# A linear-attention and gated-MLP kernel ordered anew, with one more step transposed by DMA

## The chip, the cores and the metric

The kernel runs on one core of one Trainium2 chip. A time is the device time of one execution in microseconds (us); the number that counts is the median of several runs. The core has the engines TensorE (PE, matmuls), VectorE (DVE), ScalarE (ACT), GpSimd (POOL) and SyncE (SP), which here issues nearly all DMAs. They work side by side, each through its own list of instructions in order, and wait for one another by semaphores.

## The reference

Two layers. The first is attention with a decaying state (4 batches, 8 heads, 768 positions, head size 64):

```python
for b in range(nb):                      # blocks of 64 positions
    intra = np.einsum('bhic,bhjc->bhij', qb, kb) * Dmask[None]
    intra = np.einsum('bhij,bhjd->bhid', intra, vb)
    inter = np.einsum('bhid,bhde->bhie', qb * lam_pow[None], kv_state)
    out[:, :, sl] = intra + inter
    kv_state = lam_block[None, :, None, None] * kv_state + np.einsum('bhsd,bhse->bhde', kb_dec, vb)
```

The second takes its output x (4 x 768 x 512) through a gated MLP that mixes positions:

```python
h = np.maximum(x @ w_in, 0.0)            # 512 -> 1024
u, v = (h[..., :d_ff // 2].copy(), h[..., d_ff // 2:].copy())
v_n = (v - mu) / np.sqrt(var + 1e-06)    # over the last axis
v_s = np.einsum('ts,bsd->btd', w_spatial, v_n) + b_spatial[None, :, None]
return ((u * v_s) @ w_out).astype(np.float32)
```

## The kernel before

The positions are cut into 12 steps of 256 (three to a batch; n = 0 to 11), each two chunks of 128. A step goes through these pieces; the name is the one in the table that orders them, the L number the line in the kernel before.

- Loads (LK, LQ, LV; L194): k, q and v of the step, 512 KB each, on SP's queue, into three buffers each in turn. Weights come in between (WH, WQ, WP) and are cast to bf16 (CW, CX, WC, WX).
- Scaling (KM, QM; L329): k and q times the decay, into kc and qc in bf16, on POOL or DVE. VC casts v (POOL or ACT).
- Transposing: kT and qT, two buffers each. Steps 0 to 5 do it on PE (TK, TQ; L364: eight 128x128 transposes for k and eight for q, halves of four where the piece has a half number 0 or 1, and an eviction EK or EQ). Steps 6 to 11 do it by a DMA on SP's queue (DK, L342; DQ, L346).
- Attention in 64x64 pieces of PE's array: scores (SC, L394, 16 matmuls a half), masked by DVE (MK, L399); state products (KP, L423) with the sums SX, SY, SA; outputs (AV, L457 with the state and qT, L466 with the masked scores). EX moves them to xT.
- First MLP products: PV (L491, four 512-wide matmuls a chunk) and PU (L542, eight 256-wide), evicted with the ReLU by EV and EU. BN, RA, RD, RB, VN normalise v.
- After three steps, a batch's second half: PW (L568, the spatial product, eight groups of six 384-wide matmuls, each started on a bank into which GP has put the bias), GM (DVE, the gate), PO (L579, six output tiles of four 512-wide matmuls; PH, L588, a half tile), EO and the store ST.
- FL (L307): products of a tile of ones whose results nobody reads.

What runs when is a hand-made table, ORDER, of tokens such as `SC.3.1.3.4.T`: the piece, its step and half, its PSUM banks (3 and 4) and the engine that does it (T for PE, D for DVE, A for ACT, P for POOL, S for SP). The program walks through the table once and issues each piece, so that the table gives every engine its list. Semaphore waits follow from the data. The tile `ps` is all eight PSUM banks; which bank a piece gets decides whose eviction it waits for.

Of the kernel before, what the change touches and what calls it, by code (L numbers as in the profile page):

```python
# [16 lines left out]
lam.A BR.A tab.0.A LK.0.S LQ.0.S LV.0.S LQ.1.S LK.1.S LK.2.S LV.1.S LQ.2.S WH.0.S WH.1.S posk.P idn.P msk.P one.D  # L17
row.D FL.1.256.4.1.T FL.1.512.1.1.T FL.1.256.0.1.T FL.1.256.3.1.T FL.1.256.3.1.T FL.1.512.3.1.T FL.1.512.6.1.T
LB.6.T FL.1.256.1.1.T FL.1.256.4.1.T FL.1.256.3.1.T BB.1.5.T BB.0.2.T LN.6.A LL.D mkc.D LX.A QM.0.0.P TQ.0.0.1.T
KM.0.0.D KM.0.1.D QM.0.1.P TK.0.0.0.T TK.0.1.4.T TQ.0.1.3.T EK.0.0.0.D QM.1.0.D QM.1.1.D BE.1.5.A BE.0.2.A  # L20
EQ.0.0.1.A EK.0.1.4.A VC.0.P SC.0.0.0.1.T EQ.0.1.3.A KP.0.6.T SC.0.1.4.5.T TQ.1.0.2.T TQ.1.1.3.T KM.1.1.P KM.1.0.P
MK.0.0.0.1.D KM.2.1.P KM.2.0.P VD.1.1.P TK.1.1.0.T EQ.1.0.2.A SX.0.A EK.1.1.0.A VD.1.0.A MK.0.1.4.5.D EQ.1.1.3.D
FL.1.256.2.1.T TK.1.0.1.T SC.1.1.2.3.T eps.D SY.0.6.D EK.1.0.1.D MK.1.1.2.3.D QM.2.1.P CW.0.P CW.1.P AV.0.0.6.1.T
SC.1.0.4.5.T TK.2.1.0.T TK.2.0.2.T FN.0.6.1.A SA.0.1.D AV.0.1.6.1.T KP.1.3.T EK.2.0.2.A EX.0.0.6.A MK.1.0.4.5.D
AV.1.0.2.6.T QM.2.0.D TQ.2.1.5.T TQ.2.0.4.T FN.1.2.6.A EX.0.1.1.A SA.1.0.D EK.2.1.0.D AV.1.1.2.6.T EQ.2.0.4.A
EQ.2.1.5.D SY.1.3.D CW.2.D CW.3.D EX.1.1.6.A EX.1.0.2.A SC.2.1.0.1.T SC.2.0.4.5.T PV.0.0.3.T PV.0.1.6.T PV.1.0.2.T
EV.0.0.3.A EV.0.1.6.A LV.2.S MK.2.0.4.5.D MK.2.1.0.1.D SA.1.1.D WH.3.S LK.3.S WH.2.S LQ.3.S PV.1.1.5.T VC.2.P
KP.2.6.T AV.2.0.3.6.T CX.1.D PU.1.1.4.T GP.0.0.0.0.A tab.1.A FN.2.3.6.A EV.1.0.2.A SA.2.0.D AV.2.1.3.6.T PU.0.1.1.T
EX.2.0.3.A EX.2.1.6.A KM.3.1.P KM.3.0.P BN.0.1.D BN.0.0.D EV.1.1.5.D BN.1.1.D RA.0.A GP.0.3.0.2.D BN.1.0.D
EU.1.1.4.A PV.2.0.3.T EU.0.1.1.A EV.2.0.3.A PV.2.1.6.T EV.2.1.6.A WQ.1.S WQ.0.S RD.0.D BN.2.0.D RA.1.A RD.1.D  # L30
BN.2.1.D WC.0.D WQ.2.S WC.2.D CX.0.P QM.3.1.P QM.3.0.P TK.3.2.4.T PU.0.0.3.T EK.3.2.4.A EU.0.0.3.A PU.1.0.5.T
TQ.3.2.1.T PU.2.1.6.T WC.1.P RA.2.A RB.0.D RD.2.D LQ.4.S WQ.4.S WQ.5.S WQ.3.S LV.3.S LK.4.S EQ.3.2.1.A EU.2.1.6.A
WT.1.0.4.T WT.0.0.3.T WT.2.0.1.T PU.2.0.6.T EW.0.0.3.A VN.0.0.D VN.1.1.D VN.2.0.D EW.1.0.4.D VN.1.0.D VN.0.1.D
VN.2.1.D EW.2.0.1.A EU.2.0.6.A GP.0.2.0.6.A EU.1.0.5.A WC.4.A SC.3.1.3.4.T PW.0.0.0.0.T PW.0.3.0.2.T PW.0.2.0.6.T
MK.3.1.3.4.D WC.5.D GN.2.1.P GP.0.1.1.5.D GM.0.0.0.0.D QM.4.0.P WC.3.P GM.0.2.0.6.D GM.0.3.0.2.D WT.0.1.4.T
WT.2.1.0.T WT.1.1.1.T EW.2.1.0.D EW.1.1.1.D GP.0.1.0.3.A EW.0.1.4.A GP.0.0.1.6.A QM.4.1.P KM.4.0.P KM.4.1.P WP.S
WX.0.P PW.0.1.0.3.T LV.4.S VC.4.P VC.3.A GM.0.1.0.3.D GP.0.2.1.2.A PW.0.0.1.6.T SC.3.0.0.1.T KP.3.4.T TQ.4.2.3.T
PW.0.2.1.2.T GM.0.0.1.6.D EQ.4.2.3.A WX.1.A GP.0.3.1.6.D SY.3.4.D MK.3.0.0.1.D PW.0.3.1.6.T PW.0.1.1.5.T TK.4.2.0.T
PO.0.2.3.T EO.0.2.3.A SA.3.1.D SX.3.D GM.0.2.1.2.D GM.0.3.1.6.D GM.0.1.1.5.D EK.4.2.0.D LQ.5.S QM.5.1.D QM.5.0.P
LK.5.S KM.5.0.P KM.5.1.P PO.0.0.1.T AV.3.0.2.3.T EO.0.0.1.A LV.5.S KP.4.6.T SC.4.1.4.5.T FN.3.2.3.D AV.3.1.2.3.T  # L40
SY.4.6.D SC.4.0.0.1.T PO.0.3.6.T EX.3.1.3.A TQ.5.2.3.T MK.4.1.4.5.D EQ.5.2.3.A EX.3.0.2.D PV.3.1.4.T TK.5.2.5.T
VC.5.P LK.7.S LV.6.S LK.6.S EO.0.3.6.D MK.4.0.0.1.D SA.4.0.D SA.4.1.D EK.5.2.5.A PV.3.0.2.T AV.4.0.6.3.T EV.3.1.4.A
EV.3.0.2.A FN.4.6.3.D SC.5.0.0.1.T KP.5.6.T AV.4.1.6.3.T SC.5.1.4.5.T PU.3.0.2.T EX.4.0.6.A EX.4.1.3.A PV.4.0.6.T
BN.3.1.D MK.5.0.0.1.D MK.5.1.4.5.D SA.5.0.D BN.3.0.D KM.6.0.P KM.6.1.P LQ.7.S KM.7.0.P QM.7.0.P PV.4.1.0.T
PU.4.0.1.T AV.5.0.3.4.T FN.5.3.4.D EU.3.0.2.A VC.6.A EV.4.1.0.A EV.4.0.6.A KP.6.5.T AV.5.1.3.4.T RA.3.A RD.3.D
# [596 lines left out]
```

## Time and profile before

| | before |
|---|---|
| runs | 142.14, 140.97, 142.09 us; median 142.09 |
| span of the profiled execution | 140.7 us |
| PE busy | 133.6 us (95%), 1977 matmuls |
| DVE busy | 114.0 us (81%) |
| ACT, POOL busy | 77.2 us (55%), 60.6 us (43%) |
| mean granted PE clock | 0.988 |
| moved by DMA | 34.12 MB, mean 242 GB/s |

The time of the profiled execution itself isn't listed beside its span. The span runs from its first to its last instruction; the runs were between 0.3 and 1.4 us longer. Busy shares are means over stages with different limits: in the first 17 us the loads are what everything waits for, later PE has hardly a gap.

### The profile page before, as it was taken

What the parts mean: (1) busy time and instruction counts of PE and PEld (TensorE: products, weight loads), DVE (VectorE), ACT (ScalarE), POOL (GpSimd) and SP (SyncE); (2) the same over time, 40 slices, a digit from 0 to 9 for tenths busy, and PEclk for the clock granted to TensorE, in tenths of its full rate; (3) what the DMA queues carried; (4) which work ended last, traced back from release to release, by engine and by line L of the source; (5) the groups of instructions that cost most, each with busy time, mean ns of one, the idle gap of its engine ahead of it and who ended that gap; (6) DMA issues with size and microseconds to landing.
All of it is one profiled execution on the core that took longest, in us unless ns stands there. A gap on an engine that the chain in (4) does not pass through costs nothing.

```text
span 140.7 us, 4687 instructions
## 1 busy us (share of the span) xinstructions
PE 133.6 (95%) x1977; PEld 85.6 (61%) x1977; DVE 114.0 (81%) x234; ACT 77.2 (55%) x149; POOL 60.6 (43%) x70
## 2 busy tenths in 40 slices
PE   5998879999999999999999999999999999999990
PEld 2575664778676657657666465686565666756630
DVE  1549959999989798689888978999799599985470
ACT  3264555799875369758712068684313558781111
POOL 5178664940998169900861139915802000000000
PEclk9999968999999999999999999999999999999999
DMA  3999999999999999996903799999936550025285
GB/s 84 347 347 347 386 362 363 396 373 340 368 339 317 294 271 346 236 227 202 333 26 78 166 344 372 355 229 258 158 75 57 196 203 0 5 78 220 94 303 201
DMA packets 56729, 34.12 MB, mean 242 GB/s; under 512 B 13827, under 2 KB 51971, under 8 KB 56708
## 3 DMA queue, kind: packets, MB, share of 16 engines
q1 hardware_dynamic: 56560, 33.69, 82.7%
q8 instruction: 15, 0.25, 0.7%
q10 hardware_dynamic: 148, 0.13, 0.3%
q14 instruction: 6, 0.05, 0.1%
HBM read 24.38 MB, written 6.29 MB: 218 GB/s over the span
## 4 chain that ended last, share of the span: by engine, by line
PE 84%; SPq 6%; DMA 5%; POOL 1%; issue 0%; ACT 0%; POOLq 0%
PE ps L568 22%; PE ps L491 15%; PE ps L542 15%; PE ps L579 14%; SPq L194 6%; DMA q_in<-in_q_dram 5%; PE ps L394 4%; PE ps L466 4%; PE ps L364 3%; PE ps L457 3%; PE ps L423 2%; PE ps L554 1%; POOL qc L329 1%; PE ps L588 1%; ACT o_sb L179 0%
## 5 line engine op out<-in xcount | busy, mean ns | idle before, releaser
L568 PE MATMUL ps<-wt_sb,vn 128*128 128x384 bf16 x192 | 32.9, 326 | 0.0
L399 DVE TENSOR_TENSOR a_sb<-ps,m 128x1024 bf16<-128x1024 f32 x24 | 28.5, 1215 | 2.7 <-PE ps L394 1.7
L329 POOL TENSOR_TENSOR kc<-k_in,lv 128x512 bf16<-128x512 f32 x22 | 22.9, 1063 | 14.6 <-PE ps L423 5.2
L568 PEld LDWEIGHTS <-vn 128*128 128x128 bf16 x192 | 18.4, 98 | 12.0
L329 POOL TENSOR_TENSOR qc<-q_in,lqn 128x512 bf16<-128x512 f32 x20 | 21.5, 1094 | 4.7 <-DMA q_in<-in_q_dram 4.6
L542 PE MATMUL ps<-xT,win_sb 128*128 128x256 bf16 x192 | 23.5, 273 | 0.0
L491 PE MATMUL ps<-win_sb,xT 128*128 128x512 bf16 x96 | 23.4, 384 | 0.0
L579 PE MATMUL ps<-wout_sb,gT 128*128 128x512 bf16 x92 | 21.7, 379 | 0.0
L542 PEld LDWEIGHTS <-win_sb 128*128 128x128 bf16 x192 | 18.2, 98 | 4.0 <-DVE xT L181 0.2
L574 DVE TENSOR_TENSOR gT<-ps,uT 128x384 bf16<-128x384 f32 x32 | 16.6, 551 | 3.8 <-PE ps L568 3.7
L179 ACT ACTIVATE o_sb<-ps 128x512 f32<-128x512 f32 (+1 forms) x14 | 7.6, 565 | 16.6 <-PE ps L579 10.1
L506 DVE BATCH_NORM_STATS2 st<-vh 128x6 f32<-128x512 bf16 x24 | 16.3, 680 | 0.1
L183 POOL CAST vb<-v_in 128x1024 bf16<-128x1024 f32 (+1 forms) x10 | 9.9, 995 | 13.6 <-PE ps L466 7.8
L179 ACT ACTIVATE ps<-bsp 128x384 f32<-128x384 f32 x23 | 10.9, 487 | 7.7 <-DVE gT L574 5.1
L491 PEld LDWEIGHTS <-xT 128*128 128x128 bf16 x96 | 9.0, 99 | 9.7 <-ACT xT L179 1.0
L496 ACT ACTIVATE vh<-ps 128x512 bf16<-128x512 f32 x19 | 11.1, 595 | 6.3 <-PE ps L491 5.9
L579 PEld LDWEIGHTS <-gT 128*128 128x128 bf16 x92 | 8.6, 98 | 9.2
L179 ACT ACTIVATE xT<-ps 128x512 bf16<-128x512 f32 x20 | 11.1, 593 | 5.0 <-PE ps L466 4.2
L181 DVE COPY o_sb<-ps 128x512 f32<-128x512 f32 x11 | 7.6, 688 | 4.1 <-PE ps L579 3.6
L496 ACT ACTIVATE uT<-ps 128x512 bf16<-128x512 f32 x17 | 9.8, 590 | 1.2 <-PE ps L542 1.1
L394 PE MATMUL ps<-qT,kT 64*64 64x128 bf16 x384 | 10.4, 234 | 0.0
L466 PE MATMUL ps<-a_sb,vb 64*64 64x128 bf16 x384 | 10.3, 221 | 0.1
(77 smaller groups left out, 162.2 us busy)
## 6 DMA issues: line engine op xcount, KB each, us to landing
k_in<-in_k_dram SPq DMA_DIRECT2D x12, 512.0 KB, 7.1
q_in<-in_q_dram SPq DMA_DIRECT2D x12, 512.0 KB, 6.1
v_in<-in_v_dram SPq DMA_DIRECT2D x12, 512.0 KB, 6.1
out_dram<-o_sb SPq DMA_DIRECT2D x23, 256.0 KB, 2.4
wst<-in_moe_w_in_dram SPq DMA_DIRECT2D x4, 512.0 KB, 7.6
wst<-in_moe_w_spatial_dram SPq DMA_DIRECT2D x4, 384.0 KB, 5.3
wst<-in_moe_w_out_dram SPq DMA_DIRECT2D x1, 1024.0 KB
wss<-in_moe_w_spatial_dram SPq DMA_DIRECT2D x2, 384.0 KB, 5.9
```

Of the source, the lines that this page charges most:

```text
L179: nc.scalar.activation(out=o, in_=i, func=AF.Copy)
L329: vec(e).tensor_tensor(out=dst[n % NCA][:, u].rearrange("p u m o d -> p o (u m) d"), in0=src[n % NIN].rearrange("p (o u) m d -> p o u m d" ...
L394: nc.tensor.matmul(out=pa[o][row(c), w, j], lhsT=kT[n % NTR][row(o), u, j, c * Q64:(c + 1) * Q64], rhs=qv(n, o, u, c), start=(w == 0 and j ...
L399: nc.vector.tensor_tensor(out=a_sb[n % NA][:, i].rearrange("p o w j x -> p o w (j x)"), in0=ps[:, b0:b1 + 1:b1 - b0].rearrange("p o (w y) ...
L466: nc.tensor.matmul(out=po[c ^ o][row(w), c, i], lhsT=vb[n % NCA][row(c), 4 * o + u, j, :], rhs=a[row(c), i, o, w, j, :], start=(r == 0 and ...
L491: nc.tensor.matmul(out=bank(b), lhsT=x[:, slot(c, g)], rhs=win_sb[:, g, DH:DFF], start=(g == 0), stop=(g == NCH - 1))
L496: nc.scalar.activation(out=o, in_=i, func=AF.Relu)
L506: nc.vector.bn_stats(out=st6[p2][:, t], in_=vh[p2][:, t])
L542: nc.tensor.matmul(out=pu[:, f2].rearrange("p (c x) -> p c x", c=2), lhsT=win_sb[:, g, f * P:(f + 1) * P], rhs=x[:, slot(0, g):slot(1, g) ...
L568: nc.tensor.matmul(out=bank(b)[:, 0:HW], lhsT=vn[bb % 2][:, s, f * P:(f + 1) * P], rhs=wt_sb[:, s, i * HW:(i + 1) * HW], start=False, stop ...
L574: nc.vector.tensor_tensor(out=gT[bb % 2][:, f, cols], in0=bank(b)[:, 0:HW], in1=uT[bb % 2][:, f, cols], op=ALU.mult)
L579: nc.tensor.matmul(out=bank(b), lhsT=gT[bb % 2][:, f, t * P:(t + 1) * P], rhs=wout_sb[:, f, :], start=(f == 0), stop=(f == NCH - 1))
```

## The change

Only the table changes; no function does. It is one line longer, so that each line number of the changed kernel is one higher (L394 becomes L395). All tokens are put in a new order, most PSUM banks are others, and many evictions, scalings and casts move to another engine. What can be counted:

- TK.5, TQ.5, EK.5 and EQ.5 are gone; DK.5 and DQ.5 take their place on SP.
- The products of ones are 29 instead of 11 (24 of 256 columns and 5 of 512, before 8 and 3). Before, ten of the eleven stand ahead of the first transposes; now they go on until the scores of step 2.
- PE's work in 64x64 pieces (SC, KP, AV) lies in 19 stretches instead of 20, from the first PV on in 13 instead of 16.
- By engine, before and now: EO 12 on ACT and 11 on DVE, now 18 and 5; GP 23 and 9, now 19 and 13; EQ 7 and 2, now 1 and 7; VN 7 and 17, now 3 and 21; KM 22 on POOL and 2 on DVE, now 18 and 6; RB is done 8 times before, 3 times now.

The diff, cut to two rows of the table on each side:

```diff
-VC.5.P LK.7.S LV.6.S LK.6.S EO.0.3.6.D MK.4.0.0.1.D SA.4.0.D SA.4.1.D EK.5.2.5.A PV.3.0.2.T AV.4.0.6.3.T EV.3.1.4.A
-EV.3.0.2.A FN.4.6.3.D SC.5.0.0.1.T KP.5.6.T AV.4.1.6.3.T SC.5.1.4.5.T PU.3.0.2.T EX.4.0.6.A EX.4.1.3.A PV.4.0.6.T
...
+MK.4.1.0.5.D VC.5.P GP.0.1.1.5.D GM.0.2.1.2.D PV.3.1.4.T GP.0.3.1.6.A PW.0.3.1.6.T PV.3.0.2.T PW.0.1.1.5.T DK.5.S
+DQ.5.S LV.6.S LK.6.S SA.4.0.D SA.4.1.D MK.4.0.1.3.D GM.0.3.1.6.D GM.0.1.1.5.D AV.4.0.3.6.T KP.5.0.T LQ.6.S KM.6.0.P
```

SP's queue from the v of step 5 to the transposes of step 6. The buffers are k_in_93 to 95, q_in_90 to 92 and v_in_96 to 98, one for each step modulo 3; kT_105 and qT_107 belong to even steps, kT_106 and qT_108 to odd ones. Before:

```order
26 L194 DMA v_in_98<-in_v_dram 128x8x128
27 L194 DMA k_in_94<-in_k_dram 128x8x128
28 L194 DMA v_in_96<-in_v_dram 128x8x128
29 L194 DMA k_in_93<-in_k_dram 128x8x128
30 L194 DMA q_in_91<-in_q_dram 128x8x128
31 L194 DMA q_in_90<-in_q_dram 128x8x128
32 L194 DMA q_in_92<-in_q_dram 128x8x128
33 L194 DMA v_in_97<-in_v_dram 128x8x128
34 L194 DMA k_in_95<-in_k_dram 128x8x128
35 L342 DMA_TRANSPOSE kT_105<-kc_99 128x8x128
36 L346 DMA_TRANSPOSE qT_107<-qc_101 128x8x128
```

And now, from right behind the v of step 5:

```order
28 L343 DMA_TRANSPOSE kT_106<-kc_100 128x8x128
29 L347 DMA_TRANSPOSE qT_108<-qc_102 128x8x128
30 L195 DMA v_in_96<-in_v_dram 128x8x128
31 L195 DMA k_in_93<-in_k_dram 128x8x128
32 L195 DMA q_in_90<-in_q_dram 128x8x128
33 L195 DMA q_in_92<-in_q_dram 128x8x128
34 L195 DMA k_in_94<-in_k_dram 128x8x128
35 L195 DMA v_in_97<-in_v_dram 128x8x128
36 L195 DMA q_in_91<-in_q_dram 128x8x128
37 L195 DMA q_in_90<-in_q_dram 128x8x128
38 L347 DMA_TRANSPOSE qT_107<-qc_101 128x8x128
39 L343 DMA_TRANSPOSE kT_105<-kc_99 128x8x128
```

The two transposes of step 5 stand ahead of eight loads that before had nothing but loads ahead of them.

DVE's list around the q of step 2 (qc_101 from q_in_92). Before:

```order
16 L329 TENSOR_TENSOR qc_101<-q_in_92,lqn 128x2x4x64
17 L438 TENSOR_TENSOR s_sb_113<-ps,ysb_139 128x256
18 L181 COPY kT_105<-ps 128x512
19 L181 COPY qT_107<-ps 128x512
20 L435 TENSOR_TENSOR ysb_140<-ps,ysb_139 128x256
21 L181 CAST win_sb<-wst_141 128x512 x2
22 L399 TENSOR_TENSOR a_sb_109<-ps,m_67 128x1024 x2
```

And now:

```order
16 L330 TENSOR_TENSOR qc_101<-q_in_92,lqn 128x2x4x64
17 L439 TENSOR_TENSOR s_sb_113<-ps,ysb_139 128x256
18 L212 MEMSET eps_t 128x1
19 L436 TENSOR_TENSOR ysb_140<-ps,ysb_139 128x256
20 L182 COPY qT_107<-ps 128x512
21 L182 CAST win_sb<-wst_141 128x512
22 L182 COPY qT_107<-ps 128x512
23 L439 TENSOR_TENSOR s_sb_114<-ps,ysb_140 128x256
24 L182 CAST win_sb<-wst_141 128x512
25 L400 TENSOR_TENSOR a_sb_109<-ps,m_67 128x1024 x2
```

Both halves of step 2's qT are now evicted by DVE, between the casts of w_in; two of the four casts are still DVE's.

More of the change, by code (lines that the diff above doesn't have):

```diff
@@ L16 @@
 ORDER = """
[L17 to L21, printed above, removed]
@@ L82 @@
-EO.3.1.6.A SH.3.5.0.S ST.2.2.S EO.3.4.0.D ST.3.4.S EO.3.0.5.D ST.3.0.S EO.3.2.3.D ST.3.2.S ST.3.1.S
+one.D row.D BR.A posk.P msk.P LK.0.S lam.A FL.1.256.5.1.T FL.1.256.5.1.T FL.1.256.0.1.T idn.P tab.0.A LQ.0.S
+FL.1.512.6.1.T FL.1.256.1.1.T LB.6.T FL.1.256.3.1.T LN.6.A LL.D BB.1.2.T BB.0.5.T LX.A LK.1.S KM.0.0.D KM.0.1.D LQ.1.S
+FL.1.256.4.1.T KM.1.0.P BE.0.5.A BE.1.2.A QM.0.1.D QM.0.0.D FL.1.256.1.1.T LV.0.S FL.1.256.6.1.T TK.0.0.1.T EK.0.0.1.D
+FL.1.256.3.1.T TQ.0.1.6.T TK.0.1.2.T EQ.0.1.6.D mkc.D KM.1.1.D QM.1.0.P TQ.0.0.0.T FL.1.256.1.1.T LV.1.S TK.1.0.5.T
@@ L83 @@
+PO.3.0.0.T ST.2.3.S ST.1.3.S GM.3.2.1.3.D PO.3.4.2.T EO.3.4.2.A EO.3.0.0.A PO.3.3.5.T PO.3.2.6.T PH.3.5.0.4.T
+EO.3.3.5.A EO.3.2.6.D ST.2.0.S ST.1.5.S ST.3.4.S ST.3.0.S PO.3.1.5.T ST.3.3.S EH.3.5.0.4.A EO.3.1.5.A SH.3.5.0.S
+PH.3.5.1.3.T ST.3.2.S EH.3.5.1.3.D SH.3.5.1.A ST.3.1.S
 """
```

117 lines of the change are left out of this document (59 added, 58 removed).

## The prediction

> **What bounds the kernel now.** I read the page's head and its chain first, then the chain in order of time, then the clock by stage, and last the DMA rows. The head and the shares by engine of the chain:
>
> ```profile
> span 140.7 us, 4687 instructions
> PE 133.6 (95%) x1977; PEld 85.6 (61%) x1977; DVE 114.0 (81%) x234; ACT 77.2 (55%) x149; POOL 60.6 (43%) x70
> PE 84%; SPq 6%; DMA 5%; POOL 1%; issue 0%; ACT 0%; POOLq 0%
> ```
>
> TensorE (PE) ends the time. The chain in order of time (start, length, what) says from when:
>
> ```profile
> 9.28 7.34 DMA q_in<-in_q_dram
> ...
> 16.76 1.56 POOL qc L329
> ...
> 18.37 1.03 PE ps L364 x8
> 19.40 0.36 PE ps L457 x5
> 19.75 0.43 PE ps L466 x10
> 20.18 0.85 PE ps L394 x20
> 21.04 3.96 PE ps L491 x16
> ...
> 35.24 0.35 PE ps L394 x16
> ...
> 46.10 1.73 PE ps L579 x8
> ...
> 49.25 0.97 PE ps L579 x4
> 50.22 0.45 PE ps L364 x8
> 50.67 0.86 PE ps L491 x4
> 51.53 0.45 PE ps L364 x8
> ...
> 52.84 0.24 PE ps L457 x8
> 53.08 0.22 PE ps L466 x16
> 53.30 0.22 PE ps L394 x16
> ...
> 58.41 0.25 PE ps L423 x32
> ...
> 67.11 4.87 PE ps L568 x30
> 71.98 0.57 PE ps L394 x32
> ...
> 129.98 0.44 PE ps L588 x4
> ...
> 137.13 0.02 issue
> 137.16 0.60 ACT o_sb L179
> ```
>
> Until 16.62 us (9.28 + 7.34) the loads set the pace: the q rows of step 2 are the eighth half megabyte on SP's queue. POOL scales them until 18.32, and from 18.37 to 137.13 the chain is TensorE, row upon row. So 118.8 us are a list of matmuls: whatever leaves that list, or stops running at a low clock, is saved, and any wait put into it is paid in full. The last 3.6 us are one eviction and the last stores.
>
> The clock by stage (busy us and count per engine, then granted clock, DMA share, GB/s):
>
> ```profile
> 14.60:18.00 3.40, 2.34 (x98) 1.68 (x88) 3.34 (x6) 1.78 (x5) 2.17 (x3) 1.00 1.07 386
> 18.00:21.40 3.40, 3.03 (x66) 2.39 (x67) 1.74 (x6) 1.75 (x4) 2.04 (x4) 0.56 1.12 361
> 21.40:24.80 3.40, 3.40 (x16) 1.41 (x14) 3.40 (x4) 2.07 (x4) 1.59 (x3) 0.94 1.13 369
> ```
>
> After a stretch in which PE was busy for only 2.34 of 3.40 us, the clock stood at 0.56 for the next 3.4 us, just where the list of matmuls begins: eight transposes took 1.03 us there, 0.45 at 50.22.
>
> **The change, part by part.** Terms a to e are against this execution.
>
> *a. The start.* In both orders the eighth load on SP's queue is the q of step 2, and POOL scales one half of it, so 18.32 stands. Before, what then followed was all eight q transposes, the second half of step 1's attention products (L457, L466), the scores and the w_in products, at the low clock: three of the four groups of w_in products (four matmuls each, 3.96 / 4) are done at 24.0. In the change, 18 more products of ones stand between the early pieces, the first four transposes and the attention half run before 18.3, and left are four transposes (half of 0.45), the eviction by DVE,
>
> ```profile
> L181 DVE COPY qT<-ps 128x512 bf16<-128x512 bf16 x2 | 0.8, 416 | 0.9 <-PE ps L364 0.9
> L307 PE MATMUL ps<-ones 128*128 128x256 bf16 x8 | 2.3, 393 | 1.5 <-DVE ones L303 1.5
> ```
>
> one set of scores (0.22) and three groups (0.97, then 0.86 twice): 18.35 + 0.23 + 0.45 + 0.22 + 2.69 = 21.9. ACT now casts two of the four w_in blocks behind evictions; I allow 0.5 for that: 22.4, a gain of 1.6. I take **-1.5**. Ends: nothing, if the clock drops all the same (3.4 us at half clock is about 1.5), and -2.1 without the allowance. The added ones cost nothing while PE has the wait for q before it; without that cover the four between the last k transposes and the scores of step 2 would cost 4 x 0.29 = 1.2 (2.3 / 8 each).
>
> [...]
>
> *b. Step 5's transposes.* 16 PE transposes leave, the rows at 50.22 and 51.53: 2 x 0.45 = **-0.9**, with nothing to hide behind on either side (PE has no idle there). Their two evictions leave ACT.
>
> *c. Fewer stretches.* The first 64-row group after a 128-row one takes 0.35 (35.24), a later one 0.22 (53.30); the first 128-row group after that takes 0.97 (49.25) against 0.86 (50.67; the four-matmul groups have the same size). So a stretch costs 0.13 + 0.11 = 0.24. From the first w_in products on, I count 16 stretches in the order before and 13 in the change: **-0.7**; with half the price, -0.35.
>
> *d. The end.* The last products are now half a row tile (0.44, 129.98) and the last full tile ends before it, so the last 256 KB store goes about 0.4 sooner: **-0.4**, between 0 and -0.5.
>
> *e. New waits.* The transposes of step 5 go to SP's queue, ahead of all eight loads for steps 6 to 9. The second, of q, must wait until the attention products of step 3 have read qT (same buffer) and until POOL has scaled q of step 5. DMA rows, from the SP timeline (start, issue time) and the DMA view's windows (KB, us from issue to landing), and for the q transposes from the view of their line:
>
> ```profile
> 39.65 1.39 SPq L194 DMA_DIRECT2D v_in<-in_v_dram  x1
> v_in<-in_v_dram SPq DMA_DIRECT2D x1, 512.0 KB, 6.1
> ...
> 53.23 1.39 SPq L194 DMA_DIRECT2D k_in<-in_k_dram  x1
> k_in<-in_k_dram SPq DMA_DIRECT2D x1, 512.0 KB, 6.8
> ...
> 62.67 1.00 SPq L602 DMA_DIRECT2D out_dram<-o_sb  x1
> out_dram<-o_sb SPq DMA_DIRECT2D x1, 256.0 KB, 3.3
> ...
> L346 SPq DMA_TRANSPOSE qT<-qc x6: 1240/1311/2445, 58.5 to 106.1; - x6
> DMA to landing us min/median/max: 2.9/3.5/3.8
> ```
>
> The v of step 5 lands at 45.75 (39.65 + 6.1), the k of step 8 at 60.0, the store at 66.0. Between the last two lie four transposes and the 256 KB store (0.7 us at the 361 GB/s of the window from 18.0): (6.0 - 0.7) / 4 = 1.3 us for one. In the change the same 18 loads and the weights come before step 5's transposes, so these land at 45.75 + 2 x 1.3 = 48.35. PE wants them for the scores of step 5: before at 53.30; minus a (1.5), minus b (0.9), minus three groups of the output product that now come later (1.73 + 0.97), minus one stretch: 48.0. I take a wait of **0.4**; ends 0, and 2.8 where the q transpose starts only after the k one has landed at 47.05 and then takes 3.8. [...]
>
> Step 6: eight loads (14.3 us from 45.75 to 60.0) and two transposes later, 48.35 + 14.3 + 2.6 = 65.25. PE wants them at 71.98 before; minus a, b and a stretch, minus the five groups of the spatial product that stood ahead (4.87), plus 0.4: 64.9. Wait **0.4**, ends 0 and 1.9 (a gap of 1.5 us in the loads behind the blocked queue). The scaling of step 6's k and q, on POOL and DVE, has to fit between its loads and the transposes.
>
> Steps 9 and 11: the q transpose waits for the attention products of step 7 (of 9), and PE then has 16 state products (half of 0.25), three w_in groups (2.69) and one attention half (0.46) until it wants the result, 3.3 us; in step 11 two output groups, a spatial one (4.87 / 5 = 0.97) and a w_in one, 3.7. The row says 2.9 to 3.8. Wait **0.4** together, ends 0 and 0.7. For PSUM banks now handed over by ACT and DVE around the first spatial products I add **0.3**, from 0 to 1.0. All other evictions and casts that change engine cost nothing as long as ACT (55% busy) and DVE (81%) stay ahead of PE (95%); the 0.3 is for the places where they don't. Term e is +1.5, from 0 to 6.4.
>
> The sum: -1.5 - 0.9 - 0.7 - 0.4 + 1.5 = **-2.0**. The profiled execution has a span of 140.7; its own time is not listed, and the median of the runs, 142.09, is 1.4 above that span. I take the distance as the same after: 142.1 - 2.0 = **140.1 us**.
>
> **The rivals.**
>
> 1. *The clock drops again.* [...] Against: PE work in the stretch before 18 us grows by half or so, by the ones and the attention half moved there. Term a goes to nothing: 140.1 + 1.5 = 141.6.
>
> 2. *Transposes too late: slower.* Place: the scores of step 5. If the q transpose lands 2.8 us late, PE stands still there; a gap of 1.04 us already went along with a low clock (18.37), so 1.5 us more go after it; with 0.4 in step 6, 0.7 in steps 9 and 11 and 0.3: 5.7 in waits against 3.5 in gains, 142.1 + 2.2 = 144.3. It decides from 3.5 us of waits in all. For it: this wait has 0.35 us too little room by my own sum, the queue behind it feeds step 6, and the former order had ten us of room there. Against: between step 3's attention products, which the transpose waits for, and these scores PE has three spatial and two w_in groups and more, over 5 us.
>
> 3. *No wait at all.* PE stays dense, e is 0: 138.6. For it: the former order had none after 18.4. Against: the rooms above are all under 1 us.
>
> **How the numbers follow.** Forecast 0.42 (own range 138.8 to 141.3), clock 0.15, slower 0.28, no wait 0.15. A measurement of this kernel can tell about 1% from no change: under 140.67 is faster, over 143.5 slower. Faster: 0.37 of the forecast, 0.14 of no wait, 0.02 of clock: 0.53. Slower: 0.20 of rival 2 and 0.01 of clock: 0.21. The rest, 0.26, is within 1%. The range runs from 138.2 (no wait, the larger end of a) to 144.0 (most of rival 2).
>
> **What would show it.** Right: a granted clock near 1 from 18.0 to 21.4; 80 transposes instead of 96 on PE; waits of PE on the kT and qT transposes of some tenths at steps 5, 6, 9 and 11 and nothing else long; PE's last matmul near 135.5. Wrong: PE waiting for over a us at the scores of step 5 or 6, a second stretch at half clock, or a chain that goes through DVE, ACT or POOL for several us after 20 us.

## The result, and the profile after

The changed kernel takes 163.95 us (median of five runs, 163.09 to 166.20), the kernel before 142.09 in the same comparison: ratio 1.156, 95% interval 1.151 to 1.161. Medians count all executions of a kernel, ratios leave out those more than 1.5% above its fastest. The forecast was 140.1, its range ended at 144.0. The page of the changed kernel, head and chain by engine:

```profile
span 164.5 us, 4677 instructions
PE 142.0 (86%) x1979; PEld 89.3 (54%) x1979; DVE 117.0 (71%) x226; ACT 78.7 (48%) x155; POOL 56.4 (34%) x64
PE 65%; DVE 16%; DMA 7%; ACT 5%; issue 3%; ACTq 0%; DVEq 0%
```

The profiled execution took 166.20 us; the spans of the other four are 161.4 to 162.3. The PE work is there as before (1979 matmuls, before 1977), but PE is busy for 86% of the span instead of 95%, and DVE, 0% of the chain before, is 16% of it. What PE waits for (in all, times, longest), without the 1.5 us for the tile of ones that it waits at the start in the kernel before too:

```profile
PE ps L395 <- DVE a_sb L400: 4.6, 2, 2.4
PE ps L395 <- DMA qT<-qc: 2.4, 2, 1.3
PE ps L308 <- DVE a_sb L400: 2.0, 1, 2.0
PE ps L458 <- ACT seen L180: 1.9, 1, 1.9
PE ps L492 <- DVE a_sb L400: 1.4, 1, 1.4
PE ps L395 <- DVE qT L182: 1.2, 1, 1.2
PE ps L215 <- DMA lam_in<-in_lam_dram: 1.2, 1, 1.2
```

`a_sb` is the output of the mask product MK. In the kernel before, all that the same view has of PE waiting for it is

```profile
PE ps L364 <- DVE a_sb L399: 0.2, 1, 0.2
```

Now three lines of PE wait for it by a us or more, and two of them can have no use for it: L308 (products of ones) and L492 (the w_in products) read neither `a_sb` nor anything made from it at that point. They write `ps`. The timeline of PE shows them one by one; in brackets the idle time before the row and what ended it:

```profile
15.87 0.58 PE L308 MATMUL ps<-ones 128*128 128x256 bf16 x2 [1.95 <-DVE a_sb L400]
23.04 0.31 PE L458 MATMUL ps<-qT,s_sb 64*64 64x128 bf16 x8 [1.86 <-ACT seen L180]
31.35 0.64 PE L395 MATMUL ps<-qT,kT 64*64 64x128 bf16 x16 [2.45 <-DVE a_sb L400]
51.22 0.64 PE L395 MATMUL ps<-qT,kT 64*64 64x128 bf16 x16 [2.18 <-DVE a_sb L400]
65.36 1.02 PE L492 MATMUL ps<-win_sb,xT 128*128 128x512 bf16 x4 [1.38 <-DVE a_sb L400]
```

Held against the table: the row at 31.35 is SC.2.1.1.3, which writes banks 1 and 3; the mask product it waits for, MK.2.0.0.5, reads banks 0 and 5. The row at 65.36 is PV.3.1.4, bank 4; the product is MK.4.1.0.5. At 15.87 it is a product of ones in bank 5 behind MK.0.0.2.6, at 51.22 SC.3.0.1.3 behind MK.3.1.0.2. No bank is shared in any of these pairs, but in each a bank that is written lies between the two that are read. MK reads its two banks with one strided slice:

```python
in0=ps[:, b0:b1 + 1:b1 - b0].rearrange("p o (w y) -> p o w y", w=2)
```

Before, all 24 pairs are neighbours; in the change 8 of 24 are not (banks 2 and 6, 2 and 5, 0 and 5, 1 and 3, 0 and 2, 1 and 3, 0 and 5, 1 and 3, all in steps 0 to 4). That is the first theory: the operand is waited for as the whole span from its first bank to its last. It works both ways, so that MK waits for matmuls in foreign banks too:

```profile
35.56 1.22 DVE L400 TENSOR_TENSOR a_sb<-ps,m 128x1024 bf16<-128x1024 f32 x1 [4.26 <-PE ps L492]
```

This is MK.2.1.1.3, whose scores in banks 1 and 3 were done at 31.99; it waits 4.26 us for w_in products, of which PV.1.0.2 writes bank 2. Others wait in turn (L458 at 23.04 for a sum in bank 4 that stands behind MK.1.1.2.5).

A low clock goes with the waits. Two stretches by clock (busy us and count per engine, then granted clock, DMA share, GB/s):

```profile
31.40:35.00 3.60, 3.60 (x24) 1.51 (x24) 0.00 (x0) 0.60 (x1) 1.04 (x1) 0.50 1.03 349
50.00:60.00 10.00, 8.20 (x76) 5.23 (x76) 6.04 (x11) 4.41 (x8) 4.05 (x5) 0.83 0.65 148
```

After the wait of 2.45 us at 29 to 31, PE runs its first w_in products at half the clock (0.50) for the whole stretch. The chain in order of time shows how far the list has slipped:

```profile
30.08 1.23 DVE a_sb L400
31.35 0.64 PE ps L395 x16
31.99 5.24 PE ps L492 x12
...
51.87 4.35 PE ps L569 x18
```

The first w_in product starts at 31.99 (before 21.04), the first spatial product at 51.87. SP's queue shows the two transposes of step 5 and the first load behind them:

```profile
51.96 2.04 SPq L343 DMA_TRANSPOSE kT<-kc  x1
62.30 1.24 SPq L347 DMA_TRANSPOSE qT<-qc  x1
63.60 1.84 SPq L195 DMA_DIRECT2D v_in<-in_v_dram  x1
```

The loads of step 6 begin at 63.60, before at about 42.6: a second theory, the blocked queue.

### The profile page after: what moved, and what is told of

It reads as the page before. It is cut to its first block, busy times and chain, and to the rows that moved or that the text cites. A ratio compares the mean times of both kernels' runs of the same rounds, so it can differ in the third digit from the quotient of the medians.

```text
span 164.5 us, 4677 instructions
## 1 busy us (share of the span) xinstructions
PE 142.0 (86%) x1979; PEld 89.3 (54%) x1979; DVE 117.0 (71%) x226; ACT 78.7 (48%) x155; POOL 56.4 (34%) x64
## 4 chain that ended last, share of the span: by engine, by line
PE 65%; DVE 16%; DMA 7%; ACT 5%; issue 3%; ACTq 0%; DVEq 0%
PE ps L569 15%; PE ps L492 12%; PE ps L543 10%; PE ps L580 10%; DVE a_sb L400 7%; DMA qT<-qc 6%; PE ps L395 4%; PE ps L308 3%; PE ps L467 3%; DVE vn L531 2%; PE ps L365 2%; PE ps L458 2%; PE ps L294 2%; DMA lam_in<-in_lam_dram 2%; PE ps L424 1%
## 5 line engine op out<-in xcount | busy, mean ns | idle before, releaser
L569 PE MATMUL ps<-wt_sb,vn 128*128 128x384 bf16 x192 | 34.7, 335 | 0.0
L330 POOL TENSOR_TENSOR kc<-k_in,lv 128x512 bf16<-128x512 f32 x18 | 19.0, 1065 | 35.2 <-DMA k_in<-in_k_dram 20.8
L330 POOL TENSOR_TENSOR qc<-q_in,lqn 128x512 bf16<-128x512 f32 x21 | 22.4, 1081 | 14.8 <-DMA q_in<-in_q_dram 9.3
L492 PE MATMUL ps<-win_sb,xT 128*128 128x512 bf16 x96 | 25.9, 411 | 1.4 <-DVE a_sb L400 1.4
L180 ACT ACTIVATE o_sb<-ps 128x512 f32<-128x512 f32 (+1 forms) x19 | 10.7, 581 | 15.0 <-PE ps L580 14.4
L395 PE MATMUL ps<-qT,kT 64*64 64x128 bf16 x384 | 10.4, 237 | 8.4 <-DVE a_sb L400 4.6
L492 PEld LDWEIGHTS <-xT 128*128 128x128 bf16 x96 | 9.5, 104 | 12.0 <-issue 4.5
L180 ACT ACTIVATE xT<-ps 128x512 bf16<-128x512 f32 x22 | 12.6, 596 | 6.9 <-PE ps L467 6.9
L395 PEld LDWEIGHTS <-kT 64*64 64x64 bf16 x384 | 7.4, 116 | 11.2 <-issue 9.4
L308 PE MATMUL ps<-ones 128*128 128x256 bf16 (+1 forms) x29 | 9.6, 427 | 3.5 <-DVE a_sb L400 2.0
L180 ACT ACTIVATE ps<-bsp 128x384 f32<-128x384 f32 x19 | 9.3, 497 | 2.9 <-DVE a_sb L400 2.7
```

The source lines that it names most:

```text
L180: nc.scalar.activation(out=o, in_=i, func=AF.Copy)
L308: nc.tensor.matmul(out=bank(b)[:, 0:w], lhsT=ones[:, 0:P], rhs=ones[:, 0:w], start=(new == 1 and i == 0), stop=True, skip_group_check=True)
L330: vec(e).tensor_tensor(out=dst[n % NCA][:, u].rearrange("p u m o d -> p o (u m) d"), in0=src[n % NIN].rearrange("p (o u) m d -> p o u m d" ...
L395: nc.tensor.matmul(out=pa[o][row(c), w, j], lhsT=kT[n % NTR][row(o), u, j, c * Q64:(c + 1) * Q64], rhs=qv(n, o, u, c), start=(w == 0 and j ...
L492: nc.tensor.matmul(out=bank(b), lhsT=x[:, slot(c, g)], rhs=win_sb[:, g, DH:DFF], start=(g == 0), stop=(g == NCH - 1))
L569: nc.tensor.matmul(out=bank(b)[:, 0:HW], lhsT=vn[bb % 2][:, s, f * P:(f + 1) * P], rhs=wt_sb[:, s, i * HW:(i + 1) * HW], start=False, stop ...
```

## Experiments

Line numbers differ by up to eight between these kernels; a row is told by its operation and tiles.

**1. The span of banks, and its rivals.** Four kernels, timed together with the kernel before (141.91 us there). x1_split is the changed kernel with MK as two instructions of one bank each wherever the banks are no neighbours:

```diff
     def m_k(e, n, i, b0, b1):
+        if b1 - b0 > 1:
+            for o, b in enumerate((b0, b1)):
+                nc.vector.tensor_tensor(out=a_sb[n % NA][:, i, o]..., in0=bank(b)..., in1=m01..., op=ALU.mult)
+            return
```

> The changed kernel; only where the two banks of a mask multiply (L400) are not neighbours is it done as two instructions, one for each bank, so that its operand no longer spans the banks between. Spanned banks (my theory: a strided operand over banks 2 and 6 is waited for as if it covered 2 to 6): the waits of PE on the mask multiply (4.6 + 2.0 + 1.4 + 0.3 + 0.3 us in the changed kernel) go, the second and third stretch at half clock with them, and the time falls to 146 to 155 us. Queue (rival: the spatial-weight load that waits 10.2 us on SP for the w_in casts starves PE): 160 us or more. Late order (rival: the state products of step 0 come so late that kc is not free): 160 us or more.

Measured: **150.55 us**, ratio 1.049 (1.040 to 1.058) where the changed kernel has 1.156. By the medians 13.4 of the 21.9 us are gone, by the ratios about 15 of 22. The longest waits that are left, without the one for the ones; none is for `a_sb`:

```profile
PE ps L395 <- DVE qT L182: 2.6, 3, 2.0
PE ps L395 <- DMA qT<-qc: 2.4, 2, 1.6
PE ps L215 <- DMA lam_in<-in_lam_dram: 1.5, 1, 1.5
```

x2_gap is the kernel before with its banks renamed throughout, so that 18 of the 24 pairs have one foreign bank between them and nothing else changes: 0, 1, 2, 3, 4 become 2, 4, 0, 1, 3 in every token, 5 and 6 stay.

> The kernel before with its PSUM banks renamed (0, 1, 2, 3, 4, 5, 6 become 2, 4, 0, 1, 3, 5, 6) in every token: same order, same engines, same true dependences, but 18 of the 24 mask multiplies now have one foreign bank between their two. Spanned banks: slower by 4 us or more, with new waits of PE on the mask multiply. Queue and late order: no change, 142 us within 1.

Measured: 145.72, ratio 1.024 (1.017 to 1.032): 3.4 us more by the ratio, 3.8 by the medians, a little less than the 4 that were expected. PE now waits for mask products at output products (L578) and at transposes (L363), neither of which reads them:

```profile
PE ps L578 <- DVE a_sb L398: 1.3, 1, 1.3
PE ps L363 <- DVE a_sb L398: 1.2, 3, 0.6
PE ps L465 <- DVE a_sb L398: 0.5, 2, 0.4
```

x3_wq0 is the changed kernel with the first w_spatial load, which stands waiting for a buffer at the head of SP's queue for 10 us, put further back.

```diff
-EQ.2.1.3.D WQ.0.S WH.2.S ... WQ.2.S SA.2.0.D CX.0.P WQ.1.S
+EQ.2.1.3.D WH.2.S ... WQ.2.S SA.2.0.D CX.0.P WQ.0.S WQ.1.S
```

> The changed kernel; only the first spatial-weight load on SP's queue moves five loads back, so that the w_in, spatial and v loads behind it no longer wait for the w_in casts. Queue: 157 us or less. Spanned banks: 161 to 164, since PE's first big products wait for masks and casts and not for these loads. Late order: as spanned banks.

Measured: 162.23, ratio 1.140 (1.133 to 1.148), some 2 us less than the changed kernel. The queue is not the main cause. x4_dma5 is the kernel before with only step 5's transposes changed:

```diff
-TK.5.. TQ.5.. EK.5.. EQ.5..
+LV.5.S DK.5.S ... AV.3.1.2.3.T DQ.5.S
```

> The kernel before with step 5's transposes alone given to DMA (behind the v of step 5 on SP's queue; the four PE pieces and evictions go). My terms b and e: 0.9 less work on PE and a wait of 0 to 2.8 for the transpose, since PE has only some 3.4 us of other work between step 3's attention products and step 5's scores: 141.2 to 143.5. Blocked queue (rival: the eight loads behind the transposes come late and cost step 6 its cover): 145 or more.

Measured: 146.15, ratio 1.019 (1.008 to 1.030): a loss, of 2.7 us by the ratio and 4.2 by the medians; the four executions lie between 143.71 and 147.09, too wide apart to size it better. In the profiled one (145.74) the scores of step 5 hardly wait, but the state products of step 6 do, for k:

```profile
PE ps L422 <- POOL kc L328: 2.9, 2, 2.2
PE ps L393 <- DMA qT<-qc: 0.2, 1, 0.2
```

SP's rows show why: the k transpose waits for its input until 46.0, and the load of k 6 behind it is issued at 51.01, 7 us later than before (44.07).

```profile
46.01 1.32 SPq L341 DMA_TRANSPOSE kT<-kc  x1
47.57 1.23 SPq L345 DMA_TRANSPOSE qT<-qc  x1
51.01 1.40 SPq L193 DMA_DIRECT2D k_in<-in_k_dram  x1
```

**2. The queue, the ones, and a counter-check.** Timed together, the kernel before at 141.40. y4_gap_split is x2_gap with the two-instruction MK of x1_split:

> The kernel before with its banks renamed so that 18 of 24 mask products have a foreign bank between their two (145.72 us), and these 18 done as two instructions of half the size. Theory (the operand is waited for as a span over all banks from the first to the last): with two instructions the foreign bank is free again, and the time goes back to the kernel before's, 141.5 to 142.7; the 18 more instructions on DVE cost at most some tenths. Rival (the renamed banks are bad in themselves, whatever the mask products do): 145 to 147.

Measured: 141.29, ratio 0.999 (0.996 to 1.002). With the slice gone the renamed banks cost nothing. The first theory stands: same banks, same order, only the form of the operand differs, and the ratio falls from 1.024 to 0.999, some 3.6 us. Smaller instructions could be a gain in themselves; that y4 ends at the kernel before and not below it speaks against that, but the cut alone, in neighbouring banks, was not timed.

y1_behind and y2_b_behind put the step 5 transposes by DMA behind loads of step 6 instead of ahead of them, in x1_split (shown) and in the kernel before (there behind the k of step 6, and the PE transposes go):

```diff
-PW.0.1.1.5.T DK.5.S DQ.5.S LV.6.S LK.6.S ... LQ.6.S
+PW.0.1.1.5.T LV.6.S LK.6.S ... LQ.6.S DK.5.S DQ.5.S
```

> The changed kernel with the mask product cut in two where its banks aren't neighbours (150.55 us), and besides the two transposes of step 5 issued behind the three loads of step 6 (v, k, q) instead of ahead of them. Theory (blocked queue): SP stands still from 42.9 to 45.8 and from 47.0 to 49.2 with nothing but loads behind, so these come 3 to 6 us sooner while the transposes, which wait anyway, land at about the same time; the k of step 6 is no longer waited for at about 65 us, and the time falls by 2 to 4 us, to 146.5 to 148.5. Rival (the tardiness of DVE before the first spatial product, 42.3 us against 35.6, is all that is left): DVE is as late as before, nothing changes, 150 to 151. Rival (a DMA transpose is late wherever it stands): PE waits over 2 us at the scores of step 5, and the time rises to 151.5 or more.

> The kernel before with the step 5 transposes done by DMA, issued right behind the loads of k 7, v 6 and k 6 (where the variant at 146.15 us had them ahead of these). Theory (blocked queue): the loads go as they did in the kernel before, SP waits for little, the transposes land at about 50 us, two or so before PE wants them; PE loses 16 transposes (0.9 us), the four transposes on the queue take 2.6 us from later loads: 140.5 to 142.5. Rival (the DMA transposes themselves cost, wherever they stand, since 512 KB more go through the queue while loads set the pace): 143.5 to 146, with a wait of the state products of step 6 for k as in the variant with the transposes ahead.

Measured: y1 154.00, ratio 1.088 (1.081 to 1.094) against 1.049 for x1_split: worse. y2 144.79, but as five executions from 144.62 to 145.08 at a mean clock of 0.987 or 0.988 and one of 142.48 at 0.998, so that it has no ratio: between 1.1 and 3.7 us more, by the execution. In the profiled one (144.89) the scores of step 5 wait:

```profile
PE ps L393 <- DMA qT<-qc: 2.9, 1, 2.9
```

and the chain of y2 has the transfer itself (start, length):

```profile
48.68 5.32 DMA qT<-qc
```

Issued at 48.68, the q transpose lands at 54.00, 5.3 us later. The last load ahead of it, issued at 44.18, had landed at 50.6; loads behind it were in flight too, and which of them held it up is not shown. In y1 the same line waits, twice and 3.9 us in all, the longest for 2.7. So in these orders the loads lose or the transposes lose; my expectation that the place alone mattered was wrong.

y3_ones is the kernel before with four 512-column products of ones in PE's gap of 1 us before the q transposes of step 2:

```diff
-QM.2.0.D TQ.2.1.5.T TQ.2.0.4.T
+QM.2.0.D FL.1.512.5.1.T FL.1.512.4.1.T FL.1.512.5.1.T FL.1.512.4.1.T TQ.2.1.5.T TQ.2.0.4.T
```

> The kernel before with four more products of ones of 512 columns ahead of the q transposes of step 2, in the 1.04 us in which TensorE waits for POOL there. Term a of the prediction, taken alone: the granted clock of 18.0 to 21.4 us goes from 0.56 to near 1 and the time falls by 1 to 1.5 us, to 140.4 to 140.9. [...] Rival (the ones are in the way): the clock is up but the transposes come later by the length of the ones, 141.5 to 142.5.

Measured: 141.43, ratio 0.9996 (0.9971 to 1.0021). In its profiled execution the clock is up where it was 0.56:

```profile
18.00:21.40 3.40, 3.26 (x72) 1.99 (x72) 2.67 (x7) 1.92 (x5) 2.07 (x4) 1.00 1.12 360
```

and nothing is gained. The 23 executions of the kernel before beside it say why: only 4 of them have a mean clock below 0.99 (with the ones, none of 12). As far as the mean clock tells, the stretch at 0.56 that term a wanted to remove comes in few executions, and the profiled one, with a mean of 0.988, was one of them.

**3. What else is in the changed order.** Timed together, all built on x1_split (150.55), the kernel before at 141.56: z1 without the 20 products of ones behind the first transposes; z2 with step 5 transposed on PE (into bank 0, evicted by ACT; one w_in eviction on ACT moves forward); z3 with the two copies of the mask put first on DVE, as before; z4 with all three, the w_spatial load of x3, and the q of step 0 scaled by POOL.

```diff
 z1
-FL.1.256.3.1.T ... FL.1.256.6.1.T FL.1.256.6.1.T   (20 tokens from behind TK.0.0.1.T on)
 z2
-PW.0.3.1.6.T PV.3.0.2.T PW.0.1.1.5.T DK.5.S DQ.5.S ... EV.3.1.4.A
+PW.0.3.1.6.T TK.5.2.0.T EK.5.2.0.A PV.3.0.2.T EV.3.1.4.A PW.0.1.1.5.T TQ.5.2.0.T EQ.5.2.0.A
 z3
-LX.A LK.1.S KM.0.0.D ... EQ.0.1.6.D mkc.D KM.1.1.D
+LX.A LK.1.S mkc.D KM.0.0.D ... EQ.0.1.6.D KM.1.1.D
```

> The changed kernel with the mask products cut in two (150.55 us), without the 20 products of ones that come after its first transposes. Theory (the ones have lost their cover): the list of early work on DVE ends some 4 us later than in the kernel before, so PE does the ones between pieces that are wanted; their rows between 14.2 and 24 us add up to 2.9 us, so the first w_in product comes 1 to 2.5 us sooner and the time falls to 148 to 149.5. Rival (DVE sets the pace there, the ones fill PE's waits): the first w_in product stays within 0.5 us of 25.3 and the time at 150 to 151. Rival (the ones keep the clock up): without them a stretch at half clock before the first w_in product, time 151 or more.

> The changed kernel with the mask products cut in two (150.55 us) and step 5 transposed on PE again (two times eight transposes into bank 0, evicted by ACT), so that nothing stands ahead of the loads of step 6. Theory (both places on SP's queue cost, ahead of the loads 146.15 against 141.9 in the kernel before, behind them 144.8 against 141.4): the loads of step 6 come 4 us or more sooner, the wait of DVE for the k of step 6 goes, and the time falls by 2 to 4 us to 146.5 to 148.5. Rival (what is left of the loss is the late start alone): 150 to 151.5, since 16 transposes come back to PE (0.9 us).

> The changed kernel with the mask products cut in two (150.55 us), and the copy of the mask (two instructions on DVE) put ahead of the first scaling of k, where the kernel before has it, instead of behind the first q eviction. Theory (DVE's list sets the start): the two copies took 2.05 us in DVE's way at 10.4, beside POOL, and 0.45 at the head of the list; the scores of step 0 no longer wait 2.0 us for the q eviction, and all until the first w_in product comes 1 to 2 us sooner: 148.5 to 149.7. Rival (the k of step 1 and the loads set the pace there): under 0.5 us gained, 150 to 151.

> The changed kernel with the mask products cut in two, with the three edits of this call together (no products of ones behind the first transposes, step 5 on PE, the mask copied first), the first w_spatial load put behind the third, and the q of step 0 scaled by POOL as in the kernel before. Theory (the loss is spanned banks, then the blocked queue, then a start in which DVE has too much to do): the gains add up to 5 to 8 us, 142.5 to 145.5, with the first w_in product before 22.5 us. Rival (the order as a whole is worse in its later half as well): the first w_in product comes sooner but the last matmul doesn't follow, 146.5 to 149. Rival (there is a gain beyond the kernel before): under 141.4.

Measured: z1 149.09, ratio 1.045 (1.038 to 1.052); z2 149.46, 1.053 (1.046 to 1.061); **z3 146.37**, 1.032 (1.026 to 1.038); z4 151.01, 1.052 (1.045 to 1.059). Only z3 differs from x1_split (1.040 to 1.058), and its interval just misses that one: the place of the mask copies is a second cause, of 2.4 us by the ratios and 4.2 by the medians. DVE and POOL in x1_split, the scores of PE that wait, and the same copy in z3:

```profile
10.42 2.05 DVE L239 COPY m<-mfull 64x256 bf16<-64x256 bf16 x2
9.34 2.06 POOL L330 TENSOR_TENSOR qc<-q_in,lqn 128x512 bf16<-128x512 f32 x2 [0.38 <-DMA q_in<-in_q_dram]
11.35 1.59 POOL L184 CAST vb<-v_in 128x1024 bf16<-128x1024 f32 x2
13.87 0.42 PE L395 MATMUL ps<-qT,kT 64*64 64x128 bf16 x16 [2.04 <-DVE qT L182]
```

```profile
5.46 0.45 DVE L239 COPY m<-mfull 64x256 bf16<-64x256 bf16 x2
```

The same two copies take 2.05 us beside POOL's work and 0.45 ahead of it. Behind them stands the q eviction of step 0, for which PE waits 2.04 us. In the changed kernel itself the copies take 1.31 us and this wait is 1.25. The next stretch of x1_split is at half clock, that of z3 is not; but an execution of x1_split with a mean clock of 0.999 still took 148.37, so the clock is not the whole difference:

```profile
14.60:18.00 3.40, 3.18 (x34) 2.07 (x32) 2.43 (x5) 1.71 (x3) 0.00 (x0) 0.52 1.08 392
```

```profile
14.60:18.00 3.40, 3.04 (x121) 2.14 (x116) 3.40 (x7) 2.06 (x6) 2.54 (x3) 1.00 1.08 392
```

By these rows a copy takes 1.03 us on average instead of 0.2, as long as one of the POOL instructions beside it (2.06 us for two). What in POOL's work holds the copies up is not shown.

z1 and z2 gained nothing that can be told from x1_split, though z1's median lies within what was expected; z4, meant to add them all up, lost what z3 alone had gained.

**4. Why the gains don't add up.** Timed together, the kernel before at 141.40. w1 is the kernel before with the mask copies moved behind the first k eviction; w2 is z3 without the ones, w3 is z3 with step 5 on PE, w4 is z3 with both (by the edits of z1 and z2).

```diff
-LL.D mkc.D LX.A ... EK.0.0.0.D QM.1.0.D
+LL.D LX.A ... EK.0.0.0.D mkc.D QM.1.0.D
```

> The kernel before with one edit: the copy of the mask (two instructions on DVE) put behind the first k eviction, where it meets POOL's scalings, instead of ahead of the first scaling of k. Theory (the place of this copy is what the start loses): it takes 1.3 to 2 us there instead of 0.45, all of DVE's list behind it is dense until 18 us, so the first w_in product comes 0.8 to 2 us later, and a stretch at half clock may come with it: 142.5 to 144.5. Rival (the q load sets the pace whatever DVE does): 141.2 to 142.0.

> The changed kernel with the mask products cut in two and the mask copied first (146.37 us), without the 20 products of ones behind the first transposes. Theory (ones lie on PE's path, 1.5 us saved in the variant that had them out alone): 144.5 to 146, first w_in product 0.5 to 1.5 us before 22.8. Rival (with DVE relieved the ones are covered or keep the clock up): 146.2 to 148, with a stretch of 3.4 us below 0.9 of the clock if they kept it up.

> The changed kernel with the mask products cut in two and the mask copied first (146.37 us), and step 5 transposed on PE. Theory (the queue costs what it did alone, 1.1 us, or more): 144.3 to 145.5, no wait for the transposes of step 5 and an earlier k of step 6. Rival (16 transposes on PE and their evictions cost as much as the queue gives): 146 to 147.5.

> Both edits of the two kernels beside it. If the two are independent their gains add up: 142.8 to 145. The variant at 151.01 us had these two, the mask first, the first w_spatial load moved and the q of step 0 on POOL; if the last two edits are what spoilt that one, this one stays below 146.4; if it is the two of this run together, 147.5 to 152 and again a low clock.

Measured: w1 141.28, ratio 1.001 (0.998 to 1.004): no loss. The copies take long there too,

```profile
8.72 1.24 DVE L237 COPY m<-mfull 64x256 bf16<-64x256 bf16 x2
```

but in that order PE waits 1.2 us for POOL's q of step 2 anyway. It looks as if the copy costs only where DVE sets the pace of the start. w2 145.86 (0.5 less than z3, ratio 1.025 to 1.035 against 1.026 to 1.038: no difference). w3 148.61, ratio 1.051 (1.044 to 1.059), which is 2.2 us more than z3, though no transpose of step 5 is left on the queue; neither the theory nor the rival had that. w3 alone is at the ratio of z4, so neither the w_spatial load nor POOL's q is needed to explain z4. Why step 5 on PE costs this much here stays open. w4 took 147.70 once, with a mean clock of 1.0, and 151.4 to 153.3 three times, at 0.974 to 0.977: no ratio. In its profiled execution (153.28) PE stops in the middle of a group of 32 equal products, waiting for nothing that the profile knows:

```profile
17.98 0.26 PE L430 MATMUL ps<-vb,kc 64*64 64x64 bf16 x12
21.08 0.48 PE L430 MATMUL ps<-vb,kc 64*64 64x64 bf16 x20 [2.83 <-issue]
```

In the same 3 us the DMA view has one transfer of instructions, among 1.10 MB of loads:

```profile
q1 hardware_dynamic: 1641, 1.10, 110.1%
q8 instruction: 1, 0.02, 1.8%
```

and then comes a stretch at half clock:

```profile
21.40:25.00 3.60, 3.59 (x81) 2.65 (x72) 2.56 (x9) 2.86 (x6) 2.28 (x3) 0.50 0.84 231
```

The same stop stands in the traces of z1 and w2 (1.7 us each), v2 of the next part (1.6), and z3, z4 and w3 (1.2 to 1.3). Its place goes by a count. PE has done this much, in matmuls and weight loads, before it stops in w4 and in z3:

```profile
0.00:20.00 20.00, 13.43 (x223) 9.13 (x223) 12.56 (x23) 8.29 (x17) 10.19 (x18) 1.00 0.98 304
0.00:19.00 19.00, 14.92 (x223) 9.75 (x223) 12.59 (x23) 8.18 (x16) 10.59 (x18) 1.00 0.98 305
```

It is 223 weight loads in all seven, with the 20 ones or without, though this puts the stop into another piece of the list. z3, w3, z2 and y1 have a stop of 0.6 to 1.2 us after 735 weight loads, which is 512 later. And the transfer of instructions starts at 18.73 in w4 and at 17.26 in z3, 2.35 and 2.26 us before PE goes on; in the kernel before it starts at 14.2, and PE passes that count at 16.4 with hardly a gap (0.20 us). My explanation is that a PE that gets through its many small products sooner has none left to issue until the transfer is done. It fits w2: PE goes on at 19.56 us there and at 19.52 in z3, so that the time without the ones was spent waiting. All this was read from traces; no run moved the transfer, so that the cause of the stops is not shown.

**5. The transposes on a queue of their own.** Timed together, the kernel before at 141.54. v1 is the kernel before, v2 is z3, each with the two transposes of step 5 issued by ACT (in v1 the PE transposes and their evictions go).

```diff
-EX.3.1.3.A MK.4.1.4.5.D        (v2: GP.0.3.1.6.A PW.0.3.1.6.T)
+EX.3.1.3.A DK.5.A DQ.5.A MK.4.1.4.5.D
```

> The kernel before with step 5 transposed by DMA, the two transposes issued by ACT (on a queue of their own) right behind its eviction of step 3's second attention half, at about 47 us; SP's list has neither of them, so its loads go as in the kernel before. Theory (what step 5's DMA transposes cost in the kernel before, 4.2 us ahead of the loads and 3.4 behind them, is their place in SP's order): they land by 51 us, PE wants them at 52.4, nothing waits, and PE loses 16 transposes: 140.2 to 141.2 against 141.4. Rival (ACT is held for the 1.3 us that SP's rows show for the issue of one): its evictions come 2.5 us later, PE waits on them, 142 to 144. Rival (the transposes go slower beside the loads, or slow the loads, on any queue): PE waits for them or for k of step 6 by over 1 us, 142.5 to 146.

> The changed kernel with the mask products cut in two and the mask copied first (146.37 us), with the two transposes of step 5 issued by ACT instead of SP, behind the bias of PW's group 3. Theory (SP's blocked list is a part of the 4.8 us that are left): the loads of step 6 come some 4 us sooner, 144 to 145.5. Rival (what is left is DVE's and the start's, as the variant with step 5 on PE at 148.61 suggests): 146 to 147.5. Rival (ACT is held by the issue): 147.5 to 149.

Measured: v1 150.98, ratio 1.065 (1.060 to 1.070), v2 153.12, ratio 1.086 (1.080 to 1.092). For v1 that is the third expectation, and by more than thought; for v2 none of the three had it. PE's wait at the scores of step 5 in v1:

```profile
PE ps L393 <- DMA qT<-qc: 7.7, 1, 7.7
```

the chain there:

```profile
49.62 9.56 DMA qT<-qc
```

and ACT's own rows of the two issues:

```profile
48.10 1.33 ACTq L341 DMA_TRANSPOSE kT<-kc  x1
49.62 3.23 ACTq L345 DMA_TRANSPOSE qT<-qc  x1
```

The loads went as in the kernel before, and the q transpose took 9.6 us from the start of its issue (3.2 us by itself) to its landing at 59.18, where the row of the prediction had 2.9 to 3.8. Nothing that ACT issued was ahead of it but the k transpose; what was in flight beside it were SP's loads. None of the three places tried buys back the 0.9 us of PE.

## Why the prediction was wrong

**The step that failed** is in term e: "For PSUM banks now handed over by ACT and DVE around the first spatial products I add 0.3, from 0 to 1.0. All other evictions and casts that change engine cost nothing". I looked at which engine hands a bank over, not at which banks are read together. The bank pairs of MK were in the table, and the slice that reads them in the code. What the term had at 0.3 measures 13.4 us by the medians and about 15 by the ratios (x1_split against the changed kernel), and some 3.5 us in the kernel before with one foreign bank each (x2_gap, y4_gap_split). None of the three rivals had this mechanism, so no chance in the range stood for it. Two of the prediction's own signs of being wrong came: a stretch at half clock, and a chain through DVE (16% of the span).

**Of the rest**, some 7 us by the ratios, 2.4 are the place of the mask copies (z3; 4.2 of 8.5 by the medians). The prediction let DVE's work change places for nothing "as long as ACT (55% busy) and DVE (81%) stay ahead of PE", and the start is where DVE does not: the mean over the span said nothing of it. The last 4.6 us (z3's ratio of 1.032; 4.8 by the medians) stay open. Their place is known: in z3 the first w_in product starts at 22.8 us, in y3_ones at 20.05, and PE's waits behind that come to some 2 us. Two of the stops without a releaser, of 1.25 and 0.61 us, are among these rows; what they cost was not measured. Taking out the ones (w2) or step 5's DMA (w3) did not get the time back.

**a, the start (-1.5).** Wrong, in its base: the low clock is in few executions of the kernel (4 of 23), the profiled one among them, and the ones of y3_ones gained nothing. In the change the ones did not prevent lower clocks: they stand in PE's list and wait themselves, as the row at 15.87 shows (1.95 us), and the clock was 0.50 from 31.40 to 35.00. The rival that the clock drops again (141.6) was right in its condition and far too small.

**b, 16 transposes (-0.9).** Right in itself: PE does 80 in the changed kernel, and the rows of transposes behind the first w_in product, from start to start, come to 2.0 us in x1_split against 2.7 before. In the kernel before it is more than spent by what the DMA transposes cost (2.7 us in x4 and 9.2 in v1 by the ratios, 1.1 to 3.7 in y2). In the changed order it is not: with step 5 back on PE, z2 is no faster than x1_split and w3 slower than z3.

**c, fewer stretches (-0.7).** The 13 stretches are there, the gain isn't seen: all 64-row groups behind the first w_in product take 16.1 us without PE's idle time in x1_split, 15.6 in the kernel before.

**d, the end (-0.4).** Nothing: from PE's last matmul to the end of the span it is 3.5 us in x1_split (144.36 to 147.9), as before (137.13 to 140.7, 3.6 us).

**The sum's base.** The prediction set the median of 142.09 beside the span of 140.7 and took 1.4 us as the distance. In every execution whose time and span are on record the distance is 1.7 or 1.8, so the profiled one took some 142.4 us and was slower than most. That is 0.3 us, and changes nothing in the verdict.

**e, the waits for transposes.** At steps 5 and 6 the changed kernel has none, since all else is later still. At steps 9 and 11 they come to 2.4 us instead of 0.4 (0 to 0.7): there too a transpose takes longer from issue to landing (4.4 and 4.8 us in the chain) than the 3.8 of the row. Rival 2, transposes too late at the scores of step 5, is what the profiled execution of y2 shows, where only this edit is made and the loads come first: a wait of 2.9 (I had 2.8), and 144.79 us as the median (I had 144.3). Its mechanism was right for its part; that the time came so near is in part luck, since one execution took 142.48. The 1.3 us per transpose in the sum was mis-sized for a queue with loads in flight: it came from a stretch behind the last load.

## What to carry to other kernels

Where one instruction reads two PSUM banks by a stride, choose neighbours, or cut it in two: 36 instructions of 0.68 us instead of 18 of 1.22 cost nothing measurable here, while foreign banks between the pairs cost 13 to 15 us in one order and 3.5 in another. When a table of banks is given out anew, compare for each strided operand what lies between its ends, before costing anything else. Look for a stretch at a low clock in several executions before counting on its removal (here 4 of 23 had a mean clock below 0.99), and cost a DMA transpose by one that ran with loads in flight (q's took 5.3 and 9.6 us in y2 and v1, 2.9 to 3.8 in the kernel before). Where PE stops and the profile names no releaser, count the instructions before the stop in several kernels: the equal count here (223 weight loads in seven) is what led to the transfer of instructions as a suspect.

## What was not expected of the hardware

- MK's strided operand over PSUM was waited for as everything between its first and its last bank, in both directions (PE waits up to 2.45 us to write banks that MK does not read, and MK up to 4.26 us for such writes). This is the program's doing, as far as the trace tells: the matmul at 31.35 carries a wait for a semaphore of its own, which the mask product updates at 31.31. Whether the chip would wait without it was not tried.
- A 256 KB DMA transpose of q from issue to landing: 2.9 to 3.8 us in the kernel before (steps 6 to 11), 5.3 behind loads on the same queue (y2), 9.6 beside loads on another (v1). In v1 SP's next transpose waited 1.2 us for ACT's last by the view of SP's waits, and was issued at 59.31, behind its landing at 59.18.
- Two copies on DVE: 0.45 us ahead of POOL's work (z3, the kernel before), 1.24 to 2.05 beside it (w1, the changed kernel, x1_split).
- PE stops of 1.2 to 2.8 us within a group of equal matmuls, in seven kernels at the same count of instructions (223 weight loads), 2.2 to 2.5 us after the start of a transfer of instructions, while the loads fill the DMA engines (110.1% of 16 engines in w4).
